# A seven-product scheme for the second weight matrix in five tiles of the last batch

## The chip, the cores and the metric

One core of a Trainium2 chip runs the kernel. The metric is the device time of one execution in microseconds (us). TensorE (PE) multiplies, VectorE (DVE) and ScalarE (ACT) work element by element and read TensorE's results in PSUM, GpSimd (POOL) works element by element in SBUF, and SyncE (SP) issues DMAs.

## What is computed

```python
X = np.fft.rfft(x, axis=1)                       # x: 8 x 3008 x 256
Yr = Xr @ w_r - Xi @ w_i + b_r                   # 256 x 256 weights
Yi = Xr @ w_i + Xi @ w_r + b_i
Y  = shrink(Yr, 0.01) + 1j * shrink(Yi, 0.01)    # soft threshold
y  = np.fft.irfft(Y, n=3008, axis=1)             # 24064 tokens of 256
h  = y @ w_in                                    # 256 x 2048
out = maximum(h, 0) ** 2 @ w_out                 # 2048 x 256
```

## The kernel before

The transform is done as matrix products in stages, each of which leaves its result in DRAM: Fwd (a folded first stage over 24 groups), Pair (second stage, mixing with the weights, threshold, and the first stage of the inverse, for two groups), and Back (the last inverse stage, for 188 tokens). Then comes the block of the two large products, in tiles of 500 or 504 tokens: six tiles for each of the eight batches, 48 in all, numbered t = 0 to 47. Batch 7, the last, has tiles 42 to 47. A tile is a raw tile (`raw[t]`, tag `yr`, one buffer) of 128 channels x 2 halves x 2h tokens (h = 250 or 252). The class Tokens prepares it on POOL: four sums and differences (tag `ms`, `sums`), and high and low halves of seven operands (`yt`, `split`; ACT writes the high half, POOL subtracts it to get the low one). Tag `ms` has one buffer, which is also that of the output tile `mo`.

Single-precision products are made of three matmuls: high by high, low by high, high by low. The product with w_in is already a seven-product scheme (Strassen's in Winograd's form): a Step (t, n), eight for each tile, computes four blocks of 128 hidden channels x h tokens from seven products of h columns. `first(n)` issues four products (12 matmuls into the banks psh0 and psh1) and four DVE instructions, `second(n)` three products (9 matmuls into psh2 and psh3) and two DVE clamps, then ACT squares the 1000 columns of `c` and copies them to the high half `g[0]`, and POOL subtracts it to get the low half `g[1]`, in two instructions of 500 columns. `out(j)` of the same step multiplies the two halves of g by w_out in the plain way: for each j six matmuls of 500 columns, accumulated over the whole tile in the two banks pso0 and pso1. After the last step ACT copies the two banks to `mo`, and two stores follow.

The order is written out by hand. Loop index m counts half steps, 16 for a tile and 96 (a slot) for a batch. Half step m = 2n issues first(n) and out(0) of step n - 2; m = 2n + 1 issues out(1) of step n - 2 and then second(n). The helper `then` keeps each engine's instructions of these calls in the order of the calls. Around them `jobs` holds the other work with due times: in the slot of batch b the pairs of batch b + 1 (twelve, 6.0 half steps apart), the first stage of batch b + 2, and, for each tile, its Back calls and its Tokens a tile ahead of use. These are placed by a planner with a cost model of its own, which fixes one order for each engine; the engines keep to that order. Loads on SP stand in a chain (`load_next`). The psf banks, two of the eight PSUM banks, serve Fwd, Pair and Back; in the last batch Back alone.

Of the kernel before, what the change touches and what calls it, by code (L numbers as in the profile page):

```python
# [38 lines left out]
}  # L39
MAIN = {  # L40
    "xt": 3, "xe": 1, "du": 1, "kv": 1, "kp": 1, "kq": 1, "ksh": 1, "ksl": 1, "kxl": 1, "kuh": 1, "kul": 1, "kb": 1, "yr": 1,
    "ms": 1, "mp": 1, "mu": 1, "mv": 1, "mc": 3, "nam": 1,
}
CONV = ("big", "small", "dw", "ds")
SIDE = ("ka", "kb", "kcm", "kxh", "kxl", "kp", "kq", "ke", "kv", "ksh", "ksl", "kuh", "kul", "ku")


# [6 lines left out]

A11, A12, A22, S1, S2, S3, S4 = range(7)
B11, B21, B22, T1, T3, T2, T4 = range(7)


@with_exitstack
def fnet_moe(ctx: ExitStack, tc, x, w_r, w_i, b2, w_in, w_out, bm, cm, dx, am2, a32, c32, d32, out):  # L60
# [19 lines left out]

    front, conv, six = ExitStack(), ExitStack(), ExitStack()
# [21 lines left out]
    def sub(eng, out, a, b):  # L105
        return eng.tensor_tensor(out=out, in0=a, in1=b, op=ALU.subtract)  # L106
# [386 lines left out]
    class Back:  # L493
# [7 lines left out]

        def load(self):
            tag = "du" if self.spans[0][0] else "mc"
            ps = slice(2 * self.q, 2 * self.q + 2)
            if self.b == 0:
                self.u = T("du", [M2, 2, D], F32, tag=tag)
                load_next(self.u, s3[0][:, ps])
                return
            self.u = T("du", [128, 3, D], F32R, tag=tag)
# [19 lines left out]
        def mm(self):  # L529
            if self.b == 0:  # L530
                return self.mm32()
            self.y = y = T("dy", [128, 2, W2], F32)
            for c in range(2):
                cs = slice(c * 128, c * 128 + 128)
                ps = bank([128, 2, 256])[:, :, :W2]
                pv = ps.rearrange("c j (p t) -> c j p t", p=2)
                mm = nc.tensor.matmul(pv[:, :, 0], self.u[:, 0, cs], dx_sb[:, 0], start=True, stop=False)  # L537

                with tc.issue_after(mm.ins):
                    nc.tensor.matmul(pv[:, :, 1], self.u[:, 1, cs], dx_sb[:, 0], start=False, stop=False)  # L540
                nc.tensor.matmul(ps[:, 0], self.u[:, 2, cs], dx_sb[:, 1], start=False, stop=True)  # L541
                self.done = copy(act, y[:, c], ps[:, 1])
                for n, (t, lo, hi, at) in enumerate(self.spans):
                    if n == c == 0 and t not in raw:
                        raw[t] = T("yr", [128, 2, 2 * HM], F32)
                    o = y[:, c, lo:hi] if n else raw[t][:, c, at:at + hi - lo]
                    self.cut = dve.tensor_add(out=o, in0=ps[:, 0, lo:hi], in1=y[:, c, lo:hi])  # L547


        def put(self):  # L550
            t, lo, hi, _ = self.spans[1]
# [62 lines left out]
                    then(dve, sub, dve, t4, y[:, 2], t2)  # L614


    acc = {}

    class Step:
        def __init__(self, t, n):  # L620
            self.t, self.n, self.h = t, n, tiles[t][2]
            self.end = t == len(tiles) - 1 and n == NF // 2 - 1

        def product(self, ps, a, b, terms=range(3)):
            yh, yl = yts[self.t]
# [35 lines left out]
        def second(self):  # L661
            h, c = self.h, self.c
            pc, pd = self.ps[2:]
            if self.end:
                return self.finish(pc, pd)
            if self.t + self.n:
                self.product(pc[:, 0], S4, B22)
                self.product(pc[:, 1], A22, T4)
                self.product(pd[:, 0], A12, B21)
            self.rectified(c[:, 1:3], pc, self.v)  # L670
            self.rectified(c[:, 0], pd[:, 0], self.p1)
            self.cut = last_of[dve]
# [8 lines left out]
            self.low = last_of[pool]  # L681

        def finish(self, pc, pd):
            h, c = self.h, self.c
# [14 lines left out]
                then(dve, sub, dve, g[1][:, j], c[:, j], g[0][:, j])  # L699

        def out(self, j):
            t, h, f = self.t, self.h, 2 * self.n + j
            if f == 0:
                acc[t] = [bank([128, 512], f"pso{d}") for d in range(2)]

            order = ((0, 0), (0, 1), (1, 0), (1, 1), (0, 2), (1, 2))
            for d, k in sorted(order, key=lambda p: p[0]) if self.end and j else order:
                w, g = ((0, 0), (1, 0), (0, 1))[k]
                then(
                    pe, pe.matmul, acc[t][d][:, :2 * h], wout[w][:, f, d * 128:(d + 1) * 128],  # L710
                    self.g[g][:, 2 * j:2 * j + 2].rearrange("p j h -> p (j h)"),
                    start=f == 0 and k == 0, stop=f == NF - 1 and k == 2,
                )
# [38 lines left out]
    def back_tasks(t, start):  # L752
        b, c0, h = tiles[t]
        new = range(-(-c0 // W2), -(-(c0 + 2 * h) // W2))
        jobs = []
        for j, q in enumerate(new):
            k, at = Back(b, q), start + 2.2 * j
            back_last[t] = k
            ahead = 1.6 if j == 0 and t > 1 and t % len(HALF) == 1 else 0.55 if j else 0.0
            jobs += [(at - ahead, k.load), (at + 1.6, (lambda k=k: behind(k.mm)) if t == 1 else k.mm)]  # L760
            if len(k.spans) > 1:
                jobs += [(start + 14.6, k.put)]
        k = Tokens(t)
# [179 lines left out]
    for m in range(2 * len(steps) + 4):  # L943
        b, r = divmod(m, slots)
        if r == 0 and b < B:
            jobs = [(t - slots, job) for t, job in jobs]
            if b + 1 < B:
                first, step, end = 1.0, 6.0, 7.1
                if b == 0:
                    first, step, end = 10.8, 5.25, 9.1  # L950
                    for q in range(EDGE, J):
                        jobs += [(0.4 + 1.2 * (q - EDGE), second[q].load)]
                        jobs += [(4.0 + 1.2 * (q - EDGE), lambda q=q: behind(second[q].run))]
                    jobs += [(0.6, lambda: part_load(parts[-2])), (2.6, lambda: part_load(parts[-1]))]
# [14 lines left out]
            steps[n - 2].out(1)  # L969
        if n < len(steps):  # L970
            (steps[n].second if k else steps[n].first)()
        if not k and 0 <= n - 2 < len(steps):
            steps[n - 2].out(0)
        if m in LATER:
            convert(LATER[m], steps[n])
        if m == max(LATER):
            conv.close()
            pools.update(dict.fromkeys(CONV), **dict.fromkeys(SIDE, memory(ctx, "side")))
        while jobs and jobs[0][0] < r + 1:
            jobs.pop(0)[1]()  # L980

# [96 lines left out]
```

## Time and profile before

| | |
|---|---|
| three runs | 2571.66 to 2572.54 us, median 2572.21 |
| profiled execution | 2572.81 us, of which the span from first to last instruction is 2571.0 |
| TensorE, DVE, ACT, POOL busy | 2562.1, 1814.9, 1394.1, 1658.6 us |
| granted TensorE clock | 1.00 of full speed |
| end of tile 41 (its output copies), 46, and of the program | 2315.1, 2529.1, 2571.0 us after the start |

A busy share over the whole run is an average over unlike stages. Matmuls overlap in TensorE, so the cost of one is read from the distance of their starts on the time line, not from its duration.

### The profile page before, as it was taken

To read this page: it belongs to the slowest core of one execution; us is meant where nothing else is said; L and a number is where in the kernel's file an instruction comes from. 1 tells how busy PE (TensorE), PEld (TensorE's weight loads), DVE (VectorE), ACT (ScalarE), POOL (GpSimd) and SP (SyncE) were. 2 spreads that over 40 slices of the span, in tenths; PEclk is the share of its full clock that TensorE was granted. 3 is DMA by queue.
4 is the path that set the end of the run, shared out by engine and by line. 5 is a ranking of instruction groups with operands and counts; after the bars stand their busy time and mean duration, and the time that the engine had idled before them with its cause. 6 is when DMAs were issued, how large, how long until landed. Compare 5 with 4: busy or idle time off the path is not lost.

```text
span 2571.0 us, 47075 instructions
## 1 busy us (share of the span) xinstructions
PE 2562.1 (100%) x17210; PEld 2359.8 (92%) x17210; DVE 1814.9 (71%) x3652; ACT 1394.1 (54%) x2128; POOL 1658.6 (65%) x1610
## 2 busy tenths in 40 slices
PE   9999999999999999999999999999999999999999
PEld 7899999999999999999999999999999999999998
DVE  7876766777767776687766877677776677765555
ACT  5655555555555555555555555555555554545443
POOL 1167666676657766677667676667767666756564
PEclk9999999999999999999999999999999999999999
DMA  9633332343323333233322333223332232211000
GB/s 313 194 94 90 115 93 83 94 121 105 93 68 106 103 106 103 62 108 101 119 88 70 103 115 114 85 61 111 104 115 76 70 92 87 67 54 53 27 24 17
DMA packets 181437, 244.66 MB, mean 95 GB/s; under 512 B 18056, under 2 KB 126592, under 8 KB 181208
## 3 DMA queue, kind: packets, MB, share of 16 engines
q1 hardware_dynamic: 167793, 216.38, 27.1%
q0 software_dynamic: 13280, 25.16, 4.0%
q8 instruction: 138, 2.26, 0.4%
q14 instruction: 91, 0.75, 0.1%
q10 hardware_dynamic: 135, 0.12, 0.0%
HBM read 144.20 MB, written 97.39 MB: 94 GB/s over the span
## 4 chain that ended last, share of the span: by engine, by line
PE 98%; DMA 1%; DVE 1%; ACT 0%; issue 0%; POOL 0%; SPq 0%; ACTq 0%; DVEq 0%
PE pso L560 41%; PE psh L560 36%; PE psf L303 7%; PE psf L282 3%; PE psf L336 2%; PE psf L244 2%; PE psf L468 1%; PE psf L541 1%; PE psf L540 1%; PE psf L537 1%; PE psf L366 1%; PE psf L518 1%; DMA x<-x_in 0%; PE psf L478 0%; PE psf L454 0%; DMA s<-xe 0%
## 5 line engine op out<-in xcount | busy, mean ns | idle before, releaser
L106 POOL TENSOR_TENSOR mg<-mc,mg 128x500 fp32r<-128x500 f32 (+1 forms) x766 | 988.4, 1311 | 551.3 <-ACT mg L102 460.1
L560 PE MATMUL pso<-mg,wout 128*128 128x500 f32 (+1 forms) x4608 | 1162.8, 391 | 0.0
L560 PE MATMUL psh<-yt,win 128*128 128x250 f32 (+1 forms) x8064 | 1067.2, 280 | 0.8 <-DVE mc L560 0.3
L560 PEld LDWEIGHTS psh<-yt,win 128*128 128x128 f32 x8064 | 1018.8, 189 | 30.6 <-DVE yt L106 0.6
L560 PEld LDWEIGHTS pso<-mg,wout 128*128 128x128 f32 x4608 | 821.9, 189 | 129.8
L560 ACT ACTIVATE mc<-mc 128x1000 f32<-128x1000 f32 (+1 forms) x384 | 400.5, 1043 | 550.3 <-DVE mc L560 549.2
L560 DVE CUSTOM_DVE_ANT_0 mc<-psh,mv 128x250 f32<-128x250 f32 (+3 forms) x769 | 418.8, 547 | 383.0 <-PE psh L560 338.6
L102 ACT CAST mg<-mc 128x1000 fp32r<-128x1000 f32 (+1 forms) x385 | 396.7, 1031 | 15.0 <-ACT mc L560 0.7
L560 DVE TENSOR_TENSOR mv<-psh,mu 128x500 f32<-128x500 f32 (+1 forms) x384 | 261.0, 680 | 43.5 <-PE psh L560 8.1
L303 PE MATMUL psf<-wx,kxh 128*128 128x256 f32 x1008 | 208.3, 281 | 0.0
L103 DVE COPY mp<-psh 128x250 f32<-128x250 f32 (+1 forms) x384 | 160.5, 418 | 52.9 <-PE psh L560 29.3
L215 POOL TENSOR_TENSOR xs<-xt 120x256 f32<-120x256 f32 x156 | 121.2, 798 | 79.3 <-DMA xt<-x_in 37.0
L560 DVE TENSOR_TENSOR mu<-psh,mp 128x250 f32<-128x250 f32 (+1 forms) x384 | 160.8, 419 | 12.1
L303 PEld LDWEIGHTS psf<-wx,kxh 128*128 128x128 f32 x1008 | 166.6, 189 | 2.7
L324 DVE TENSOR_TENSOR kv<-psf,ke 64x256 f32<-64x256 f32 x336 | 141.5, 421 | 38.9 <-PE psf L303 26.8
L560 DVE CUSTOM_DVE_ANT_0 mc<-psh,mp 128x250 f32<-128x250 f32 (+1 forms) x384 | 157.2, 409 | 6.1 <-PE psh L560 6.0
L102 ACT COPY dy<-psf 128x188 f32<-128x188 f32 (+2 forms) x229 | 70.0, 316 | 151.7 <-PE psf L541 150.9
L106 POOL TENSOR_TENSOR ksl<-kv,ksh 128x512 fp32r<-128x512 f32 x84 | 108.7, 1294 | 51.8 <-ACT ksh L102 51.6
L303 PE MATMUL psf<-wx,kxl 128*128 128x256 f32 x504 | 141.8, 281 | 0.0
L547 DVE TENSOR_TENSOR yr<-psf,dy 128x188 f32<-128x188 f32 (+2 forms) x224 | 69.0, 314 | 80.4 <-ACT dy L102 77.5
L106 POOL TENSOR_TENSOR yt<-yr,yt 128x250 fp32r<-128x250 f32 (+1 forms) x94 | 88.2, 940 | 45.7 <-ACT yt L102 45.5
L106 DVE TENSOR_TENSOR xl<-xs,xh 120x512 fp32r<-120x512 f32 x78 | 113.4, 1454 | 1.7 <-ACT xh L102 1.7
(127 smaller groups left out, 2647.7 us busy)
## 6 DMA issues: line engine op xcount, KB each, us to landing
du<-s SPq DMA_DIRECT2D x112, 256.0 KB, 2.8
ka<-s SPq DMA_DIRECT2D x96, 256.0 KB, 3.1
kcm<-cm_in POOLq DMA_DIRECT2D x84, 256.0 KB, 3.7
s<-kuh SPq DMA_DIRECT2D x84, 256.0 KB, 2.9
s<-kul SPq DMA_DIRECT2D x84, 256.0 KB, 3.5
s<-xe SPq DMA_DIRECT2D x82, 240.0 KB, 2.4
xt<-x_in SPq DMA_DIRECT2D x81, 240.0 KB, 3.2
out<-mo SPq DMA_DIRECT2D x64, 250.0 KB, 2.3
```

Of the source, the lines that this page charges most:

```text
L102: return act.copy(out=out, in_=in_)
L103: return eng.tensor_copy(out=out, in_=in_)
L106: return eng.tensor_tensor(out=out, in0=a, in1=b, op=ALU.subtract)
L215: return eng.tensor_tensor(out=out[:, :n], in0=self.xt[:, :n, 0], in1=self.xt[:, :n, 1], op=(ALU.add, ALU.subtract)[t])
L244: nc.tensor.matmul(ps[:, t], am_sb[0][:, j, t], v[:, t], start=n == 0, stop=n == 2)
L282: nc.tensor.matmul(pv[:, :, c, g, :], self.a[:, g, c * 128:(c + 1) * 128], bg, start=True, stop=True)
L303: self.last = nc.tensor.matmul(ps, l, wx[j][:, k, c, :], start=n == 0, stop=n == 5)
L324: dve.tensor_add(out=v[64 * r:64 * r + 64, g], in0=ps[gs], in1=self.e[gs, r])
L336: nc.tensor.matmul(ps[:, g], self.cm[:, g, j * 128:(j + 1) * 128], r[:, g], start=n == 0, stop=n == 2)
L366: self.mm = nc.tensor.matmul(ps[:M1, t], nam if t and i else am32[:, t], self.xt[:, 0, i], start=i == 0, stop=i == 1)
L547: self.cut = dve.tensor_add(out=o, in0=ps[:, 0, lo:hi], in1=y[:, c, lo:hi])
L560: last_of[eng] = op(*args, **kwargs)
```

## The change

For tiles 42 to 46 (`FREE`), steps 1, 3 and 5 of the eight (`SEVEN`) multiply by w_out with the seven-product scheme as well: `out_seven` issues 21 matmuls of h columns. The new operands are four sums of blocks of w_out for each of the three steps (`out_sums`, on POOL, once, in slot 6), and four sums of blocks of g for each such step (`forms`: three DVE instructions on `c` after its squaring, then high halves on ACT and low halves on POOL). Two of the seven products go straight to the pso banks and three parts into the two psf banks, which the tile keeps from step 1 on; `tile_sums` combines them on DVE after the next tile's step 0 has begun, and the final result is added to the pso banks by DVE where ACT copied them before. To have the psf banks free, all 16 Back calls of batch 7 are done in slot 6 (from half step 68.5 on), the columns of tiles 43 to 47 are stored to DRAM (`y7`), and each of these tiles is loaded again a tile ahead of its use. The pairs of batch 7 are 5.25 half steps apart instead of 6.0, and the buffers of the pair stage are given up at 68.5 for the new ones.

```diff
+ENDS = B - 1
+FREE = range(ENDS * len(HALF), B * len(HALF) - 1)
+SEVEN = (1, 3, 5)
...
     # Back.load
+            if self.b == ENDS:
+                tag = ("th", "tl")[self.q % 2]
...
     # Back.mm
-                    if n == c == 0 and t not in raw:
+                    kept = t in FREE[1:] or t > FREE[-1]
+                    if n == c == 0 and t not in raw and not kept:
                         raw[t] = T("yr", [128, 2, 2 * HM], F32)
-                    o = y[:, c, lo:hi] if n else raw[t][:, c, at:at + hi - lo]
+                    o = y[:, c, lo:hi] if n or kept else raw[t][:, c, at:at + hi - lo]
...
+            if self.b == ENDS and self.spans[-1][0] > FREE[0]:
+                lo = min(lo for t, lo, _, _ in self.spans if t > FREE[0])
+                nc.sync.dma_start(y7[:, :, W2 * self.q + lo:W2 * (self.q + 1)], y[:, :, lo:])
...
+    def out_sums(n):
...
+        pool.tensor_add(out=st[:, :512].rearrange("p (f d) -> p f d", f=2), in0=wout[0][:, 2 * n:2 * n + 2], in1=wout[1][:, 2 * n:2 * n + 2])
+        a11, a21, a12, a22 = w[:, 0, 0], w[:, 0, 1], w[:, 1, 0], w[:, 1, 1]
+        pool.tensor_add(out=s[:, 0], in0=a21, in1=a22)
+        sub(pool, s[:, 1], s[:, 0], a11)
+        sub(pool, s[:, 2], a11, a21)
+        sub(pool, s[:, 3], a12, s[:, 1])
+        halves(ws[0][:, i], ws[1][:, i], s, pool)
+
+    def tile_sums(t):
...
+        o = T("mo", [128, 4 * HM], F32, tag="ms")[:, :4 * h]
...
+        then(dve, copy, dve, s[:, 0], p16[:, 0])
+        then(dve, dve.tensor_add, out=u, in0=p16[:, 1], in1=s[:, 0])
+        then(dve, dve.tensor_add, out=s[:, 1:3], in0=p57, in1=u.unsqueeze(1).broadcast_to([128, 2, h]))
+        then(dve, dve.tensor_add, out=s[:, 3], in0=p57[:, 0], in1=s[:, 2])
...
     # Step.second
-            for j in (slice(0, 2), slice(2, 4)):
+            for j in (slice(0, 1), slice(2, 4)) if self.seven else (slice(0, 2), slice(2, 4)):
                 then(pool, sub, pool, g[1][:, j], c[:, j], g[0][:, j])
...
+        def forms(self):
...
+            then(dve, sub, dve, s[:, 0:2], c[:, 1::2], c[:, 0:2])
+            then(dve, dve.tensor_add, out=s[:, 2], in0=c[:, 0], in1=s[:, 1])
+            then(dve, sub, dve, s[:, 3], c[:, 2], s[:, 2])
+            for j in (slice(0, 2), slice(2, 4)):
+                then(act, copy, act, self.th[:, j], s[:, j])
+                then(pool, sub, pool, self.tl[:, j], s[:, j], self.th[:, j])
+
+        def out_seven(self, j):
...
+            if j == 0:
+                todo = ((p16[:, 0], plain[0], g, 0), (low[:, 0], plain[1], g, 2), (low[:, 1], sums[3], g, 3))
+            else:
+                todo = (
+                    (p57[:, 0], sums[0], tf, 0), (p57[:, 1], sums[2], tf, 1),
+                    (p16[:, 1], sums[1], tf, 2), (high[:, 0], plain[2], tf, 3),
+                )
+            for at, (ps, a, b, k) in enumerate(todo):
+                for q, (x, y) in enumerate(((0, 0), (1, 0), (0, 1))):
+                    then(
+                        pe, pe.matmul, ps, a[x], b[y][:, k],
...
     # Step.out, after the last step of a tile
-                    if d and self.end:
+                    if t in FREE:
+                        then(dve, dve.tensor_add, out=o[:, d], in0=acc[t][d][:, :2 * h], in1=o[:, d])
+                    elif d and self.end:
...
+    def raw_load(t):
+        _, c0, h = tiles[t]
+        raw[t] = T("yr", [128, 2, 2 * HM], F32)
+        load_next(raw[t][:, :, :2 * h], y7[:, :, c0:c0 + 2 * h])
+
+    def last_tasks(start, step):
+        jobs = [(start, late)]
+        for q in range(S // W2):
+            k = Back(ENDS, q)
+            jobs += [(start + 1.0 + step * max(q - 2, 0), k.load), (start + 2.6 + step * q, k.mm)]
+        return jobs + [(start + 2.0 + 5.0 * j, lambda n=n: out_sums(n)) for j, n in enumerate(SEVEN)]
...
     # the loop over half steps
+                if b + 1 == ENDS:
+                    step = 5.25
+                    jobs += last_tasks(68.5, 1.6)
                 jobs += pair_tasks(pairs[b + 1], first, step, end)
...
             (steps[n].second if k else steps[n].first)()
+            if not k and n and steps[n - 1].seven:
+                steps[n - 1].forms()
+            if not k and n % (NF // 2) == 0 and steps[n].t - 1 in FREE:
+                tile_sums(steps[n].t - 1)
```

## Rows read from the trace of the kernel before

**Rows 1.** The page, part 1: busy us, share of the span, instructions.
```profile
PE 2562.1 (100%) x17210; PEld 2359.8 (92%) x17210; DVE 1814.9 (71%) x3652; ACT 1394.1 (54%) x2128; POOL 1658.6 (65%) x1610
```

**Rows 2.** The page, part 4: the chain that ended last, by engine.
```profile
PE 98%; DMA 1%; DVE 1%; ACT 0%; issue 0%; POOL 0%; SPq 0%; ACTq 0%; DVEq 0%
```

**Rows 3.** Stretches of tiles 41, 46: busy PE, PEld, DVE, ACT, POOL; clock, DMA.
```profile
2315.10:2359.40 44.30, 44.30 (x290) 40.40 (x289) 25.85 (x58) 22.32 (x32) 29.01 (x28) 1.00 0.16 48
...
2487.80:2529.10 41.30, 41.30 (x265) 37.59 (x264) 23.51 (x48) 18.87 (x21) 24.54 (x23) 1.00 0.04 13
```

**Rows 4.** Time line, a step of tile 46: start, duration, instruction, [idle before <-releaser].
```profile
2508.44 2.60 PE L560 MATMUL psh<-yt,win 128*128 128x250 f32 x21
2509.33 0.68 DVE L560 CUSTOM_DVE_ANT_0 mc<-psh,mv 128x500 f32<-128x500 f32 x1 [1.81 <-PE psh L560]
...
2510.87 2.88 PE L560 MATMUL pso<-mg,wout 128*128 128x500 f32 x12
...
2511.41 0.68 DVE L560 TENSOR_TENSOR mv<-psh,mu 128x500 f32<-128x500 f32 x1
2511.49 1.03 ACT L102 CAST mg<-mc 128x1000 fp32r<-128x1000 f32 x1
2512.26 0.42 DVE L560 CUSTOM_DVE_ANT_0 mc<-psh,mv 128x250 f32<-128x250 f32 x1 [0.17 <-DVE mv L560]
2512.60 2.50 POOL L106 TENSOR_TENSOR mg<-mc,mg 128x500 fp32r<-128x500 f32 x2 [2.67 <-ACT mg L102]
...
2513.59 2.60 PE L560 MATMUL psh<-yt,win 128*128 128x250 f32 x21
```

**Rows 5.** Groups by line and form, POOL, 2359 to 2530 (busy us, mean ns).
```profile
L106 POOL TENSOR_TENSOR mg<-mc,mg 128x500 fp32r<-128x500 f32 x50 | 62.4, 1269 | 45.5 <-ACT mg L102 44.2 <-DVE mc L560 1.3
...
L106 POOL TENSOR_TENSOR yt<-yr,yt 128x250 fp32r<-128x250 f32 x3 | 2.2, 733 | 0.4 <-ACT yt L102 0.3
```

**Rows 6.** Groups by line and form, ACT, 2359 to 2530.
```profile
L102 ACT CAST yt<-ms 128x500 fp32r<-128x500 f32 x8 | 4.9, 612 | 4.5 <-POOL ms L106 4.5
```

**Rows 7.** Groups by line and form, DVE, whole run.
```profile
L106 DVE TENSOR_TENSOR xl<-xs,xh 120x512 fp32r<-120x512 f32 x78 | 113.4, 1454 | 1.7 <-ACT xh L102 1.7
...
L106 DVE TENSOR_TENSOR kxl<-psf,kxh 128x512 fp32r<-128x512 f32 x84 | 57.6, 685 | 35.7 <-ACT kxh L102 34.9
...
L215 DVE TENSOR_TENSOR xu<-x 120x256 f32<-120x256 f32 x6 | 2.3, 421 | 0.0
```

**Rows 8.** Time line, 446 to 449: POOL and DVE.
```profile
446.52 2.96 POOL L106 TENSOR_TENSOR mg<-mc,mg 128x504 fp32r<-128x504 f32 x2 [1.93 <-ACT mg L102]
...
447.09 1.26 DVE L106 TENSOR_TENSOR xl<-xs,xh 120x512 fp32r<-120x512 f32 x1
```

**Rows 9.** Time line, 781 to 788: POOL and DVE.
```profile
781.83 0.73 POOL L106 TENSOR_TENSOR kxl<-kp,kxh 128x256 fp32r<-128x256 f32 x1
781.84 5.31 DVE L106 TENSOR_TENSOR xl<-xs,xh 120x512 fp32r<-120x512 f32 x1
...
785.33 1.26 POOL L106 TENSOR_TENSOR yt<-ms,yt 128x504 fp32r<-128x504 f32 x1
```

**Rows 10.** Time line, 2445 to 2459: the end of tile 44.
```profile
2445.16 1.06 ACT L102 COPY mo<-pso 128x500 f32<-128x500 f32 x2 [1.18 <-PE pso L560]
...
2446.09 0.68 DVE L560 CUSTOM_DVE_ANT_0 mc<-psh,mv 128x500 f32<-128x500 f32 x1 [1.98 <-PE psh L560]
...
2448.67 1.31 POOL L106 TENSOR_TENSOR ms<-yr 128x250 f32<-128x250 f32 x2 [2.12 <-DMA out<-mo]
...
2452.39 0.63 POOL L576 TENSOR_TENSOR ms<-yr,ms 128x250 f32<-128x250 f32 x1
2452.97 1.07 POOL L106 TENSOR_TENSOR yt<-ms,yt 128x500 fp32r<-128x500 f32 x1
2454.00 0.73 POOL L106 TENSOR_TENSOR ms<-yr,ms 128x250 f32<-128x250 f32 x1
```

**Rows 11.** Groups by line, TensorE, whole run: one of three lines of Back.
```profile
L541 PE MATMUL psf<-dx_sb,du 128*128 128x188 f32 x224 | 58.5, 273 | 0.2 <-DMA du<-s 0.2
```

More of the change, by code (lines that the diff above doesn't have):

```diff
@@ L41 @@
     "xt": 3, "xe": 1, "du": 1, "kv": 1, "kp": 1, "kq": 1, "ksh": 1, "ksl": 1, "kxl": 1, "kuh": 1, "kul": 1, "kb": 1, "yr": 1,
-    "ms": 1, "mp": 1, "mu": 1, "mv": 1, "mc": 3, "nam": 1,
+    "ms": 1, "mp": 1, "mu": 1, "mv": 1, "mc": 3, "nam": 1, "wsh": 1, "wsl": 1, "tt": 1, "th": 2, "tl": 2,
 }
 CONV = ("big", "small", "dw", "ds")
+LATE = ("wsh", "wsl", "tt", "th", "tl")
 SIDE = ("ka", "kb", "kcm", "kxh", "kxl", "kp", "kq", "ke", "kv", "ksh", "ksl", "kuh", "kul", "ku")
@@ L68, in fnet_moe @@
     s3 = [dram.tile([M2 + M2 if b else M2, NP, D], F32, name=f"s3_{b}") for b in range(B)]
+    y7 = dram.tile([128, 2, S], F32, name="y7")
     am32 = const.tile([M1, 2, M1], F32, name="am32")
@@ L78, in fnet_moe @@
     dx32 = const.tile([M2, 2 * N2], F32, name="dx32")
-    front, conv, six = ExitStack(), ExitStack(), ExitStack()
+    front, conv, six, side = ExitStack(), ExitStack(), ExitStack(), ExitStack()
     def memory(stack, name, **kwargs):
@@ L508, in load @@
                 return
-            self.u = T("du", [128, 3, D], F32R, tag=tag)
+            if self.b == ENDS:
+                self.u = T("du", [128, 1024], F32R, tag=tag)[:, :3 * D].rearrange("p (k d) -> p k d", k=3)
+            else:
+                self.u = T("du", [128, 3, D], F32R, tag=tag)
             load_next(self.u[:, :2].bitcast(F32), s3[self.b][:128, ps])
@@ L614, in begin @@
                     then(dve, sub, dve, t4, y[:, 2], t2)
-    acc = {}
+    acc, part, last_sums = {}, {}, {}
+    ws = []
+    def out_sums(n):
+        if not ws:
+            ws.extend(T(name, [128, len(SEVEN), 4, 128], F32R) for name in ("wsh", "wsl"))
+        i = SEVEN.index(n)
+        st = T("st", [128, 1024], F32, tag="tt")
+        w = st[:, :512].rearrange("p (f e d) -> p f e d", f=2, e=2)
+        s = st[:, 512:].rearrange("p (j d) -> p j d", j=4)
+        pool.tensor_add(out=st[:, :512].rearrange("p (f d) -> p f d", f=2), in0=wout[0][:, 2 * n:2 * n + 2], in1=wout[1][:, 2 * n:2 * n + 2])
[6 more added lines that the diff above has]
+    def tile_sums(t):
+        h = tiles[t][2]
+        p16, p57 = part.pop(t)
+        o = T("mo", [128, 4 * HM], F32, tag="ms")[:, :4 * h]
+        s = o.rearrange("p (j h) -> p j h", j=4)
+        u = T("mu", [128, HM], F32)[:, :h]
+        then(dve, copy, dve, s[:, 0], p16[:, 0])
+        then(dve, dve.tensor_add, out=u, in0=p16[:, 1], in1=s[:, 0])
+        then(dve, dve.tensor_add, out=s[:, 1:3], in0=p57, in1=u.unsqueeze(1).broadcast_to([128, 2, h]))
+        then(dve, dve.tensor_add, out=s[:, 3], in0=p57[:, 0], in1=s[:, 2])
+        last_sums[t] = o.rearrange("p (d h) -> p d h", d=2)
     class Step:
@@ L622, in __init__ @@
             self.end = t == len(tiles) - 1 and n == NF // 2 - 1
+            self.seven = t in FREE and n in SEVEN
         def product(self, ps, a, b, terms=range(3)):
@@ L678, in second @@
             self.bent = last_of[act]
-            for j in (slice(0, 2), slice(2, 4)):
+            for j in (slice(0, 1), slice(2, 4)) if self.seven else (slice(0, 2), slice(2, 4)):
                 then(pool, sub, pool, g[1][:, j], c[:, j], g[0][:, j])
             self.low = last_of[pool]
+        def forms(self):
+            h, c = self.h, self.c
+            s, self.th, self.tl = [
+                T(f"f{name}", [128, 1024], dt, tag=name)[:, :4 * h].rearrange("p (j h) -> p j h", j=4)
+                for name, dt in (("tt", F32), ("th", F32R), ("tl", F32R))
+            ]
+            then(dve, sub, dve, s[:, 0:2], c[:, 1::2], c[:, 0:2])
[5 more added lines that the diff above has]
+        def out_seven(self, j):
+            t, h, n = self.t, self.h, self.n
+            i = SEVEN.index(n)
+            if i == j == 0:
+                part[t] = [bank([128, 512])[:, :2 * h].rearrange("p (j h) -> p j h", j=2) for _ in range(2)]
+            low, high = [a[:, :2 * h].rearrange("p (j h) -> p j h", j=2) for a in acc[t]]
+            p16, p57 = part[t]
+            f = 2 * n
+            plain = [[w[:, f + k, d * 128:(d + 1) * 128] for w in wout] for d, k in ((0, 0), (0, 1), (1, 1))]
+            sums = [[w[:, i, k] for w in ws] for k in range(4)]
+            g, tf = self.g, (self.th, self.tl)
+            if j == 0:
+                todo = ((p16[:, 0], plain[0], g, 0), (low[:, 0], plain[1], g, 2), (low[:, 1], sums[3], g, 3))
+            else:
+                todo = (
[6 more added lines that the diff above has]
+                        pe, pe.matmul, ps, a[x], b[y][:, k],
+                        start=i == q == at == 0, stop=i == len(SEVEN) - 1 and q == 2 and j == 1 and at in (1, 2),
+                    )
         def finish(self, pc, pd):
@@ L701, in out @@
         def out(self, j):
+            if self.seven:
+                return self.out_seven(j)
             t, h, f = self.t, self.h, 2 * self.n + j
@@ L715, in out @@
                 b, c0, _ = tiles[t]
-                o = T("mo", [128, 4 * HM], F32, tag="ms")[:, :4 * h].rearrange("p (d h) -> p d h", d=2)
+                if t in FREE:
+                    o = last_sums.pop(t)
+                else:
+                    o = T("mo", [128, 4 * HM], F32, tag="ms")[:, :4 * h].rearrange("p (d h) -> p d h", d=2)
                 for d in range(2):
-                    if d and self.end:
+                    if t in FREE:
+                        then(dve, dve.tensor_add, out=o[:, d], in0=acc[t][d][:, :2 * h], in1=o[:, d])
+                    elif d and self.end:
                         then(act, copy, act, o[:, d, :h], acc[t][d][:, :h])
@@ L754, in back_tasks @@
         new = range(-(-c0 // W2), -(-(c0 + 2 * h) // W2))
+        if b == ENDS:
+            new = ()
         jobs = []
@@ L762, in back_tasks @@
                 jobs += [(start + 14.6, k.put)]
+        if t > FREE[0]:
+            jobs += [(start, lambda: raw_load(t))]
         k = Tokens(t)
@@ L770, in back_tasks, with late @@
         return jobs
+    def raw_load(t):
[8 more added lines that the diff above has]
+        return jobs + [(start + 2.0 + 5.0 * j, lambda n=n: out_sums(n)) for j, n in enumerate(SEVEN)]
+    def late():
+        side.close()
+        pools.update(dict.fromkeys(LATE, memory(ctx, "late")))
     def at(items, n, *names):
@@ L977, in fnet_moe @@
             conv.close()
-            pools.update(dict.fromkeys(CONV), **dict.fromkeys(SIDE, memory(ctx, "side")))
+            pools.update(dict.fromkeys(CONV), **dict.fromkeys(SIDE, memory(side, "side")))
         while jobs and jobs[0][0] < r + 1:
```

## The prediction

> **What bounds the kernel now.** I read the page's busy times first, then its chain of waits, then the last batch tile by tile, then one step on the time line. TensorE is busy for 2562.1 of 2571.0 us, and no other engine is over 71% [rows 1]; the chain that ended last lies on TensorE for 98% [rows 2]. In the stretches of tiles 41 and 46 TensorE is busy for the whole of 44.30 and 41.30 us at a granted clock of 1.00 (its 2.4 GHz level), POOL for 29.01 and 24.54 [rows 3]. So TensorE's instruction stream sets the end, there is no stall to win back, and each new wait of TensorE counts in full. The time line of tile 46 says how late an operand may come [rows 4]. The 21 psh matmuls of 250 columns (nine of second(n), then twelve of first(n+1)) issue from 2508.44 to 2510.87, 0.1157 us each; the twelve pso matmuls of 500 columns from 2510.87 to 2513.59, 0.2267 us each. A step is 2.43 + 2.72 = 5.15 us.
>
> Measured from the end of second(n) on TensorE (2508.44 + 9 x 0.1157 = 2509.48): ACT's copy to the high half ends at 2511.49 + 1.03, 3.04 after; POOL's low halves run from 2512.60, 3.12 after, 1.25 us each; DVE has finished first(n+1) at 2512.26 + 0.42, 3.20 after [rows 4]. TensorE wants the first low half at 1.39 + 2.72 + 2.43 (first, out, then 21 psh) plus four matmuls, 7.45 after; POOL has it at 4.37. These 3.1 us are the slack of the step before the change.
>
> **What the change takes away on TensorE.** A seven-product step issues 9 + 12 = 21 matmuls of 250 columns where twelve of 500 stood: 12 x 0.2267 - 21 x 0.1157 = 0.29 us. There are 3 steps in each of 5 tiles: 15 x 0.29 = 4.4 us. The inverse stage of the last batch issues the same matmuls as before, earlier: nothing on TensorE.
>
> **What it adds, and where that lies.** In a seven-product step POOL has one low half of 250 columns (0.73, [rows 5]) in place of 500, and then two low halves of the differences, tl, of 1.25 each. These wait for ACT's high halves th (0.61, [rows 6]), and those for the three DVE instructions of forms(), which stand behind first(n+1) on DVE and can't start before 3.20. TensorE wants the first tl at 1.39 + 2.72 + 2.43 + 9 x 0.1157 + 2 x 0.1157 = 7.81, the second at 7.81 + 6 x 0.1157 = 8.51: the slack of 3.1 us is spent on a longer chain.
>
> The price that decides is that of forms(): its instructions read two operands from SBUF. Such an instruction on 512 columns takes 1454 ns on average while its twin with one operand in PSUM takes 685 ns [rows 7]. The time line shows why: at 447.09 the DVE subtraction starts under a POOL instruction that runs from 446.52; it ends 1.26 us later, 0.58 us after that POOL instruction (446.52 + 1.25 = 447.77), and POOL's pair takes 2.96 instead of the 2.50 us of an undisturbed pair [rows 4, 8]. So the DVE instruction waits for the running POOL instruction, then holds POOL up by 0.46. One on 250 columns is 685 - 421 = 0.26 us shorter [rows 7], so I take 0.20 for it. And forms() starts at 3.20, just when POOL starts its low halves at 3.12.
>
> One rule speaks against the change. The Trainium skill, "SBUF — State Buffer", section "Who interferes with whom", says that a DVE instruction with two SBUF inputs and a GpSimd instruction that reads SBUF exclude each other for a whole instruction, and that one SBUF input does not. By that rule a DVE instruction waits for at most one POOL instruction, and the sum would be the one below. The trace agrees at 447.09 but goes further at 781.84: there one subtraction took 5.31 us, and five POOL instructions ran to their end before it [rows 8, 9]; by that row a single one of the 45 forms() instructions could cost several us.
>
> *Step 5, POOL otherwise idle.* Low half 3.12 to 3.85; the first difference gets in at 3.85 and ends at 4.43; POOL's next low half 4.31 to 5.56; the second difference, which needs the first, waits to 5.56; tl one 5.76 to 7.01, in time for 7.81; the third difference waits for that, ends at 7.33; ACT to 7.94; tl two 7.94 to 9.19 where 8.51 was wanted: TensorE waits 0.68 us.
>
> *Step 1, behind the tile's end.* The final adds move from ACT (at 2445.16) to DVE: 2 x 0.68 from 2445.16 ends at 2446.52, the clamps of second() started at 2446.09 [rows 10], so they and the low halves come 0.43 later, at 3.55. On POOL the next tile's two differences ms (1.31) run ahead of them as they do now (2448.67, when the store of mo has landed, 2.4 us after its copies, [rows 10]); 0.30 later than now they end at 4.04. From there as above: low halves 4.50 and 5.43 to 6.68, tl one 6.88 to 8.13 (0.32 late), tl two to 9.38, a further 0.55 late: 0.87 us.
>
> *Step 3.* POOL still owes the next tile 0.63 + 1.07 + 0.73 and a second 1.07 = 3.5 us of sums and splits [rows 10]. Between step 2's low halves and step 3's, idle time for some 2.1 us of it is left; I take 0.68 as in step 5 and 0.2 for the overhang. If all of it goes ahead, 1.4 us more.
>
> A tile: 0.87 + 0.88 + 0.68 = 2.43 us late, less 3 x 0.29 = 0.87 won: 1.56 us slower; five tiles 7.8.
>
> **Costed at nothing, with what hides it.** tile_sums: 0.42 + 0.42 + 0.68 + 0.42 = 1.94 us on DVE (durations of the same shapes, [rows 4]) in a gap of 1.81 before the next clamp; 0.1 late, inside 3.1 us of slack; without that cover it would be 0.1 a tile. It and the adds have an operand in PSUM, so POOL isn't held. out_sums: three times about 4.6 us of POOL (two instructions of 512 columns at 1.27 and four of 128, each under the 0.63 of a 250 one, [rows 5, 10]) in tiles 40 and 41, where POOL idles 15.3 of 44.3 us [rows 3]; one instruction ahead of a low half is 1.27 late against 3.1. Without cover: 14 us. The reload of a tile is issued once the previous raw tile has been read, over 10 us ahead of its use; a store of half its size lands in 2.4 us [rows 10]. The pairs of the last batch come 5.25 half steps apart instead of 6: the same matmuls.
>
> The inverse stage goes into the last third of slot 6: three loads and a store each on SP, two copies on ACT, two to four additions on DVE, two psf banks. Raw tile 42 has one buffer, which tile 41's Tokens still read until about half step 75 of the slot, so the additions of the first Back wait there with both psf banks; queued behind them are later Backs, whose place on TensorE the planner chooses. On SP a Back load that waits for one of its four buffers, or a reload that waits for the raw tile, holds the stores of mo queued behind it, and these hold ms on POOL; the four buffers put each load three Backs ahead. The nearest row: all 224 such matmuls of the run waited 0.2 us for their data [rows 11]. Bounds 0.2 and 3 us (one POOL instruction late, 1.27, on a bank or two); I take 0 in the sum, nearest to the row, and keep 3 for the range.
>
> **The sum.** The profiled run took 2572.81 us, 1.8 over its span and 0.6 over the median of 2572.21. 2572.8 - 4.4 + 5 x 2.43 = 2580.6; I say 2580.5, 0.3% slower.
>
> **The rivals.**
> *The slack holds*: if forms() gets its three instructions in without waiting (0.68 + 0.42 + 0.42 from 3.20 ends at 4.72, tl two at 3.12 + 0.73 + 3 x 1.25 = 7.6, before 8.51), nothing is late and the time is 2572.8 - 4.4 = 2568.4. For it: 685 ns is what such an instruction takes when POOL happens to be between instructions. Against it: POOL has work back to back from 3.12 to 7.6 in every such step. It decides where a wait is under 0.3 us a step.
> *Step 1 alone is late*: if the arbitration lets DVE's second and third difference follow the first at one boundary, steps 3 and 5 are in time (0.46 + 0.20 + 0.20 added to 7.6 is 8.46), and step 1 loses about 0.9: 2572.8 - 4.4 + 5 x 0.9 = 2572.9, no change.
> *POOL's backlog*: all 3.5 us of the next tile go ahead of tl in step 3, and steps 1 and 5 as above: 1.4 - 0.2 us more a tile, 2580.6 + 6 = 2586.6; with lost arbitrations as at 781.84, 2590.
> *Faster by more than 0.2%*: that is 5.1 us, about what a measurement of this kernel can tell from no change; the matmuls give 4.4, so something else would have to end earlier, and no row shows what could.
>
> **Chances.** Forecast (2577.5 to 2585) 0.46; slack holds 0.20; step 1 alone 0.18; backlog 0.13; faster 0.03. Both middle cases lie within 0.2%: faster 0.03, same 0.38, slower 0.59. The range from 2568.4 to 2590 takes in all but the ends of the last two; the forecast's own is 2577.5 to 2585.
>
> **What would show it.** In tiles 42 to 46: twenty-one matmuls of 250 columns in place of twelve of 500 in out() of steps 1, 3 and 5; TensorE waiting for POOL's tl, 0.5 to 1 us each, some 12 us in all; forms() instructions of 0.8 to 1.8 us instead of 0.42 to 0.68; POOL low halves of about 1.7. It is wrong if the forms() instructions take their undisturbed time, if TensorE waits for something else in those tiles, or if the stretch of tiles 37 to 41 grows by more than its moved inverse stage of 13 x 6 matmuls.

## The result, and the profile after

The changed kernel takes 2586.28 us (median of four runs, 2585.36 to 2586.48); the kernel before, run beside it, 2572.38. The ratio is 1.0054 with a 95% interval of 1.0036 to 1.0071: 13.9 us slower, 5.8 us above the forecast and 1.3 us above the forecast's own range. The profiled execution took 2586.48 us with a span of 2584.7.

The page, parts 1 and 4:
```profile
PE 2567.2 (99%) x17345; PEld 2369.2 (92%) x17345; DVE 1869.0 (72%) x3727; ACT 1407.5 (54%) x2151; POOL 1706.7 (66%) x1653
...
PE 96%; DVE 2%; POOL 1%; DMA 1%; ACT 0%; issue 0%; SPq 0%; DVEq 0%; POOLq 0%; ACTq 0%
```
Against [rows 1, 2] DVE's and POOL's shares of the chain have grown from 1 and 0% to 2 and 1%, and TensorE is busy 5.1 us longer though its stream was to be 4.4 us shorter. Both have to be explained, so the next view is the last batch tile by tile: stretches from one tile's first output addition to the next, for tiles 42 to 46 (busy PE, PEld, DVE, ACT, POOL; granted clock, DMA).
```profile
2321.36:2366.34 44.98, 42.97 (x292) 39.96 (x291) 34.92 (x61) 23.39 (x28) 34.93 (x31) 0.96 0.08 24
2366.34:2409.91 43.57, 41.39 (x292) 38.39 (x291) 36.08 (x63) 22.31 (x26) 34.45 (x31) 1.00 0.08 25
2409.91:2454.19 44.28, 42.61 (x292) 39.88 (x291) 34.67 (x64) 22.20 (x26) 33.75 (x31) 0.96 0.08 25
2454.19:2498.46 44.27, 42.62 (x292) 39.89 (x291) 34.60 (x64) 22.18 (x26) 33.57 (x31) 0.96 0.08 24
2498.46:2542.77 44.31, 42.60 (x292) 39.87 (x291) 34.23 (x64) 21.39 (x24) 32.06 (x29) 0.96 0.04 13
```
Tile 46 took 41.30 us with TensorE always busy [rows 3]; now 44.31 with 1.7 us of idle. Tile 43 alone has a clock of 1.00, and a TensorE busy time that is at least 1.2 us shorter than its neighbours'. So two things are lost: idle time, and clock.

The view of waits of TensorE, 2322 to 2543 us, has one line (total, times, longest):
```profile
PE psf L574 <- POOL ftl L112: 9.1, 11, 1.6
```
Every wait is for POOL's low half of the differences (tl in the code, ftl in the trace; ftt are the three results of forms(), fth their high halves). Counted from one matmul's start to the next, less its usual 0.117, and with the 0.10 us by which the matmul after each wait is late too, the eleven waits come to 2.70, 2.97, 2.20, 2.19 and 2.24 us in tiles 42 to 46: 12.3. Step 1 has 2.32, 2.18, 2.20, 2.19 and 2.24 of it, step 3 0.39 and 0.79 in tiles 42 and 43 and nothing later, step 5 nothing. The view's 9.1 us are idle time alone; the other 3.2 us are counted as busy, since a matmul that starts late is drawn longer.

Step 1 of tile 46 on the time line (start, duration, instruction, [idle before <- releaser]):
```profile
2498.46 1.26 DVE L574 TENSOR_TENSOR mo<-pso,mo 128x500 f32<-128x500 f32 x2 [0.83 <-PE pso L574]
...
2502.06 1.31 POOL L112 TENSOR_TENSOR ms<-yr 128x250 f32<-128x250 f32 x2 [2.04 <-DMA out<-mo]
...
2503.24 0.67 DVE L112 TENSOR_TENSOR ftt<-mc 128x500 f32<-128x500 f32 x1
2503.32 2.59 POOL L112 TENSOR_TENSOR mg<-mc,mg 128x250 fp32r<-128x250 f32 x2
...
2503.95 0.83 DVE L574 TENSOR_TENSOR ftt<-mc,ftt 128x250 f32<-128x250 f32 x1
...
2504.81 1.37 DVE L112 TENSOR_TENSOR ftt<-mc,ftt 128x250 f32<-128x250 f32 x1
2505.87 0.81 POOL L590 TENSOR_TENSOR ms<-yr,ms 128x250 f32<-128x250 f32 x1
...
2506.64 1.07 POOL L112 TENSOR_TENSOR yt<-ms,yt 128x500 fp32r<-128x500 f32 x1
...
2507.67 2.46 POOL L112 TENSOR_TENSOR ftl<-ftt,fth 128x500 fp32r<-128x500 f32 x2
...
2508.96 0.38 PE L574 MATMUL psf<-ftl,wsh 128*128 128x250 f32 x1 [1.46 <-POOL ftl L112]
...
2510.18 0.38 PE L574 MATMUL psf<-ftl,wsh 128*128 128x250 f32 x1 [0.25 <-POOL ftl L112]
...
2510.75 4.15 PE L574 MATMUL psh<-yt,win 128*128 128x250 f32 x21
```
Up to POOL's low halves (mg) the order is as forecast: the additions on DVE, the two ms ahead of mg, and mg ended 6.39 us after second(n) had ended on TensorE (2498.48 + 9 x 0.1157 = 2499.52), forecast 6.68. But between mg and the first ftl stand 0.81 + 1.07 us of the next tile's sums and split; the forecast had those two behind ftl. Without them the first ftl would have been there 1.8 us earlier, and the wait that it causes is 1.62 us (2508.96 - 2507.22 - 0.12). The last line is the second loss: 21 psh matmuls reach from 2510.75 to the next out at 2514.74, 3.99 us where they took 2.43 [rows 4]. The stretches around it show why (same columns as above):
```profile
2509.00:2510.72 1.72, 1.47 (x10) 1.27 (x11) 0.41 (x1) 0.23 (x1) 1.72 (x2) 1.00 0.00 0
2510.72:2514.13 3.41, 3.41 (x18) 3.41 (x17) 1.06 (x2) 1.39 (x2) 3.41 (x4) 0.50 0.02 5
2514.13:2520.00 5.87, 5.87 (x41) 5.40 (x40) 5.35 (x10) 2.65 (x5) 3.38 (x4) 1.00 0.00 0
```
For 3.41 us the granted clock is at its 1.2 GHz level, right behind step 1's two waits (in tile 42 from the end of the second wait on). The same happens in tiles 42, 44 and 45, not in 43; each time some 1.56 us, four times 6.2. The sum by the trace: 2572.8 - 4.4 + 12.3 + 6.2 = 2586.9, where the profiled run took 2586.48. TensorE's busy time follows too: -4.4 + 6.2 + 3.2 = 5.0 us longer.

Step 5 of tile 46, where the forecast had 0.68 us of waiting and there is none:
```profile
2526.49 2.67 POOL L112 TENSOR_TENSOR mg<-mc,mg 128x250 fp32r<-128x250 f32 x2 [1.92 <-ACT mg L108]
2529.12 2.67 POOL L112 TENSOR_TENSOR ftl<-ftt,fth 128x500 fp32r<-128x500 f32 x2
...
2526.49 0.67 DVE L112 TENSOR_TENSOR ftt<-mc 128x500 f32<-128x500 f32 x1
2527.20 0.83 DVE L574 TENSOR_TENSOR ftt<-mc,ftt 128x250 f32<-128x250 f32 x1
2528.06 1.37 DVE L112 TENSOR_TENSOR ftt<-mc,ftt 128x250 f32<-128x250 f32 x1
```
DVE's first difference starts in the same instant as POOL's first low half and runs its undisturbed 0.67; POOL's is the one held up, 1.26 us where 0.73 is undisturbed. The other two differences follow at the next boundaries of POOL, one POOL instruction earlier than reckoned, so that the second ftl follows the first at once.

### The profile page after: what moved, and what is told of

Same layout as the page of the kernel before. It is cut to its first block, busy times and chain, and to the rows that moved or that the text cites. A ratio compares the mean times of both kernels' runs of the same rounds, so it can differ in the third digit from the quotient of the medians.

```text
span 2584.7 us, 47574 instructions
## 1 busy us (share of the span) xinstructions
PE 2567.2 (99%) x17345; PEld 2369.2 (92%) x17345; DVE 1869.0 (72%) x3727; ACT 1407.5 (54%) x2151; POOL 1706.7 (66%) x1653
## 4 chain that ended last, share of the span: by engine, by line
PE 96%; DVE 2%; POOL 1%; DMA 1%; ACT 0%; issue 0%; SPq 0%; DVEq 0%; POOLq 0%; ACTq 0%
PE pso L574 39%; PE psh L574 36%; PE psf L309 7%; PE psf L288 3%; PE psf L342 2%; PE psf L250 2%; PE psf L474 1%; PE psf L552 1%; PE psf L551 1%; PE psf L548 1%; PE psf L574 1%; PE psf L372 1%; POOL ftl L112 1%; PE psf L529 1%; PE psf L409 0%; PE psf L484 0%
## 5 line engine op out<-in xcount | busy, mean ns | idle before, releaser
L574 PE MATMUL pso<-mg,wout 128*128 128x500 f32 (+2 forms) x4473 | 1123.2, 390 | 0.0
L574 PEld LDWEIGHTS pso<-mg,wout 128*128 128x128 f32 x4473 | 796.5, 189 | 126.1
L332 ACT ACTIVATE kc<-kv,low 128x512 f32<-128x512 f32 x84 | 60.9, 725 | 100.4 <-DVE kv L330 100.3
```

Of the source, the lines that this page charges most:

```text
L332: act.activation(r, v, AF.Relu, bias=low)
L574: last_of[eng] = op(*args, **kwargs)
```

## The experiments

The theory after the result: nothing is lost but by TensorE waiting for ftl, because POOL comes late (its own backlog in step 1, DVE's differences between its instructions), and by what the clock does after such a wait. Rivals: the moved inverse stage costs something of its own; DVE's extra work, not POOL's order, is the cause; the clock is only a symptom that costs nothing more.

**The move alone.** The inverse stage of the last batch runs early and is kept in DRAM, and all steps use the plain scheme.
```
-            self.seven = t in FREE and n in SEVEN
+            self.seven = False
```
(with it go out_sums, tile_sums and the final additions).


> The inverse stage of the last batch is moved and kept in DRAM as in the change, the product with w_out stays plain everywhere. If the cost lies in the seven-product steps alone (POOL late with the low halves of the differences, and TensorE's clock after the long wait): 2572.4 us as before, within 1 us, and no wait of TensorE over 0.3 us in tiles 36 to 46. If the move costs too (banks held in the last third of slot 6, reloads): 1 to 3 us more than before.


Measured: 2572.26 us, ratio 1.0001 (0.9991 to 1.0010). Tile 46, same columns as in [rows 3]:
```profile
2486.98:2528.27 41.29, 41.29 (x265) 37.57 (x264) 23.51 (x48) 18.84 (x21) 24.55 (x23) 1.00 0.04 13
```
The move costs and brings nothing; all of the 13.9 us lies in the seven-product scheme, that is its steps, out_sums, tile_sums and the final additions.

**Steps 3 and 5 alone.** `SEVEN = (3, 5)`.


> Seven-product scheme in steps 3 and 5 only. If the order on POOL behind the tile's end (the next tile's sums and split ahead of the differences) is what makes step 1 late, steps 3 and 5 have small waits: 10 x 0.29 = 2.9 us won, less 0 to 0.3 us a step, so 2569.5 to 2572.5, clock at full speed throughout. If the exclusion between DVE's and POOL's instructions alone costs 0.68 us in every seven-product step, as the prediction's step 5 has it: 2572.4 - 2.9 + 10 x 0.68 = 2576.3.


Measured: 2573.01 us, 1.0005 (0.9996 to 1.0014): between the two expectations. TensorE's waits:
```profile
PE psf L574 <- POOL ftl L112: 2.4, 5, 0.5
```
Step 3 waits 0.61 to 0.67 us, and 0.10 behind it, in each tile; step 5 never does; the clock stays at 1.00. So at full clock step 3 costs about what the forecast said (0.72 to 0.77 against 0.88) and step 1 is the heavy one. The sum closes: 2572.1 less 10 x 0.29, plus 5 x 0.74, is 2572.9.

**The forms left out.** The three DVE differences are not made; th and tl come from c, so the output lacks them.
```
-            then(dve, sub, dve, s[:, 0:2], c[:, 1::2], c[:, 0:2])
-            then(dve, dve.tensor_add, out=s[:, 2], in0=c[:, 0], in1=s[:, 1])
-            then(dve, sub, dve, s[:, 3], c[:, 2], s[:, 2])
+            s = c
```


> The three DVE instructions of forms are left out: ACT and POOL split blocks of c itself instead of the four sums, so the output lacks them; the matmuls are as in the change. If DVE's waiting for POOL, and POOL's for DVE, are a main part of the lateness: waits of some 0.7 us in step 1 only (POOL still has the next tile's differences first), clock at full speed, 2572.4 - 4.4 + 3.3 = 2571.3. If POOL's own work is enough to make it late, the waits stay near 2 us a tile and the time over 2580.


Measured: 2569.82 us, 0.9990 (0.9981 to 1.0000). What is left are waits of 0.29 to 0.36 us in step 1 of each tile. POOL's low half of 250 columns, from the groups by form, and tile 46:
```profile
L112 POOL TENSOR_TENSOR mg<-mc,mg 128x250 fp32r<-128x250 f32 x9 | 6.6, 729 | 7.2 <-ACT mg L108 7.2
...
2485.23:2526.13 40.90, 40.70 (x292) 38.16 (x291) 26.44 (x54) 20.75 (x24) 30.30 (x29) 1.00 0.04 14
```
In the changed kernel the same group takes 1049 ns on average: a difference on DVE holds POOL up. TensorE's saving shows here: 40.90 - 0.46 of waits = 40.44, against 41.29 above, is 0.85 us a tile where 0.87 was reckoned. In step 1 POOL's order changed with this edit too (the split yt came behind ftl), so there it doesn't part the differences from the order. In step 3 POOL's instructions stand in the order of the changed kernel, and no wait is left; with the differences it is 0.61 to 0.67 us (steps 3 and 5 alone), so that wait is made by them.

**The next tile's sums and splits behind step 1's ftl**, by hand, with everything else as in the changed kernel.
```
...
+            jobs += [(start + 7.1 + j, lambda j=j: later(steps[8 * (t - 1) + 1].differences, lambda: k.sums(j)))]
...
```


> The next tile's sums and differences are queued on POOL behind the low halves of step 1's differences; POOL's order is otherwise the planner's (in step 3 it puts one split of 1.07 us between the two low halves). If POOL's order in step 1 decides: the wait of step 1 falls from 2.2 us to about 0.5, step 3 gets about 1 us, no single wait over 1.2 us, clock at full speed: 2572.4 - 4.4 + 5 x 1.5 = 2575.5. If the exclusion between DVE and POOL decides, step 1 keeps 1.5 us or more and the time stays over 2580.


Measured: 2578.71 us, 1.0025 (1.0016 to 1.0035): between the two expectations; 7.6 us of the 13.9 come back by the order, in part because the clock falls once only, for 6.83 us in tile 42. TensorE's waits:
```profile
PE psf L574 <- POOL ftl L112: 5.2, 11, 1.5
PE pso L574 <- POOL mg L112: 0.2, 1, 0.2
```
Step 1's wait is at most 0.21 us in four tiles of five (0.94 in tile 46), but step 3 now waits 0.85 to 2.0: what POOL still owes comes there. In tile 44's step 3 one difference lost several boundaries in a row:
```profile
2423.21 1.11 POOL L112 TENSOR_TENSOR yt<-ms,yt 128x500 fp32r<-128x500 f32 x1
...
2423.73 3.71 DVE L112 TENSOR_TENSOR ftt<-mc 128x500 f32<-128x500 f32 x1
2424.24 0.76 POOL L112 TENSOR_TENSOR ms<-yr,ms 128x250 f32<-128x250 f32 x1
2424.92 1.98 POOL L112 TENSOR_TENSOR mg<-mc,mg 128x250 fp32r<-128x250 f32 x2
...
2429.52 0.38 PE L574 MATMUL psf<-ftl,wsh 128*128 128x250 f32 x1 [0.88 <-POOL ftl L112]
```
It started under yt and ended only after four POOL instructions, 3.71 us, as the 5.31 us of [rows 9] did.

**The second half of a seven-product step half a step later**, so that ftl has more time (and tile_sums half a step later with it).
```
-            steps[n - 2].out(1)
+            if not steps[n - 2].seven:
+                steps[n - 2].out(1)
...
+            if n > 2 and steps[n - 3].seven:
+                steps[n - 3].out(1)
...
```


> The second half of a seven-product step (the four products that read th and tl) is issued one half step later, behind the first half of the next step's plain product, and the sums of a tile accordingly half a step later: 3.8 us more time for tl. If the lateness of tl is the whole loss (with the clock after it), no wait is left and 2572.4 - 4.4 = 2568.0 us. If something else in the scheme costs (DVE's load, POOL's total), it stays above 2572.


Measured: 2579.41 us, 1.0028 (1.0017 to 1.0039), not the 2568.0 that was expected if ftl's lateness were the whole loss. No wait for ftl is left, but two others are:
```profile
PE pso L574 <- POOL mg L112: 3.8, 5, 1.0
PE psh L574 <- DVE mc L574: 2.3, 5, 0.5
```
POOL's backlog isn't gone by being waited for later: the plain low half of step 2 is now what is late, and DVE's clamps, which stand behind the differences, are late for the transforms that follow.

**Both of these edits.**


> Both edits together: the next tile's sums and differences behind tl of step 1 on POOL, and the second half of a seven-product step half a step later. If POOL's backlog in steps 1 to 3 is the loss, and each edit alone only moved it (to step 3, or to step 2's plain low halves), both together leave waits of under 0.5 us a tile: 2572.1 - 4.4 + 2 = 2569.7 or less. If DVE, held up by POOL in forms, is late for psh as well (some 1 us a tile with the second half late alone): 2573 to 2575.


Measured: 2577.01 us, 1.0019 (1.0010 to 1.0027), above both expectations.
```profile
PE pso L574 <- POOL mg L112: 3.5, 5, 1.1
PE psh L574 <- DVE mc L574: 1.9, 4, 0.5
```
The wait for DVE's clamps stays in four tiles; the one for a plain low half has moved from step 2 to step 4. In tile 46 POOL works without a gap from 2496.32 until the low half of step 4 has come at 2515.03. Three seven-product steps in eight leave POOL no room from step 1 to step 4, whichever instruction is late.

**The matmuls that read only high halves first.** In the second half of each such step the eight matmuls with fth go ahead of the four with ftl; POOL's order is left.
```
...
+            if j:
+                terms.sort(key=lambda term: term[1] == 2)
...
```


> Within the second half of a seven-product step the eight matmuls that need only high halves go first, then the four that read tl. POOL's order is that of the change. tl comes 9.44 and 10.66 us after the end of second() in step 1 of tile 46; the wait of 1.6 and 0.4 us becomes two of about 0.95 us each, and the step ends 0.23 us earlier. If the half-speed clock follows from the one long wait, it is gone: 2586.3 - 6.2 - 1.2 = 2579. If it follows from the sum of the waits, it stays and the time is 2585.


Measured: 2581.43 us, 1.0037 (1.0022 to 1.0051), between the two expectations. Step 1 waits 0.86 to 1.11 and then 0.87 us, step 3 0.40 to 0.44 in the four tiles at full clock. The clock fell in one tile of five instead of four; TensorE's waits, and tiles 44 and 46:
```profile
PE psf L574 <- POOL ftl L112: 8.5, 14, 0.9
...
2407.70:2451.70 44.00, 42.54 (x292) 39.82 (x291) 34.52 (x64) 22.18 (x26) 33.79 (x31) 0.96 0.08 25
2494.68:2537.70 43.02, 41.26 (x292) 38.33 (x291) 35.62 (x63) 21.38 (x24) 32.68 (x29) 1.00 0.04 13
```
Counted from start to start as above, its waits come to 12.2 us, as in the changed kernel (12.3). Three slow stretches fewer should then save 3 x 1.56 = 4.7 us; the time is 4.9 us less. So the clock has a price of its own, beside that of the waits.

**The wait filled with work.** To part the clock from the wait, matmuls that add zero to a bank stand ahead of the first ftl matmul of step 1, thirteen of them, then six in a second kernel.
```
+                    if i == 0 and j and at == 0 and q == 2:
+                        for _ in range(13):
+                            then(pe, pe.matmul, ps[:, :128], zero, zero, start=False, stop=False)
```


> In step 1, ahead of the first matmul that reads tl, TensorE issues 13 matmuls of 128 zero columns into the same sum (1.46 us, adding zero): the wait is filled with work, the operands come as late as in the change. If the stretches at half clock (3.41 us each in four tiles, 21 psh matmuls in 3.99 instead of 2.43 us) are a cost of TensorE's pause, they go: 2586.3 - 4 x 1.56 = 2580.1. If the waits alone account for the loss and the clock does not matter, 2586 or more.

> As the filled wait before, with 6 zero matmuls in place of 13: each runs as two passes of 0.11 us, so 13 filled 2.82 us where 1.6 were open and gave the clock's gain back; 6 fill 1.3 us. If the half-speed stretches cost 4 x 1.56 us and need TensorE's pause: full speed throughout and 2586.3 - 6.2 = 2580.1. If the clock costs nothing of its own: 2586.


Measured: 2586.00 us (1.0054) with thirteen, 2583.99 us (1.0046, 1.0030 to 1.0061) with six. In both the clock stays at 1.00 in all tiles. The thirteen took longer than the wait they fill (each runs as two, 26 recorded in a tile, some 2.8 us), so that kernel tells nothing on the price. With six, tile 46 and its step 3 (POOL's low halves, then the matmul that waits):
```profile
2496.60:2540.11 43.51, 42.62 (x304) 39.70 (x303) 35.62 (x63) 21.39 (x24) 32.62 (x29) 1.00 0.04 13
...
2515.39 1.44 POOL L112 TENSOR_TENSOR ftl<-ftt,fth 128x500 fp32r<-128x500 f32 x1
...
2517.82 1.26 POOL L112 TENSOR_TENSOR ftl<-ftt,fth 128x500 fp32r<-128x500 f32 x1 [1.00 <-ACT fth L108]
...
2519.14 0.39 PE L574 MATMUL psf<-ftl,wsh 128*128 128x250 f32 x1 [0.49 <-POOL ftl L112]
```
Step 3 waits 0.61 to 0.67 us in every tile again, as it does with steps 3 and 5 alone and, with 0.69, in tile 43 of the changed kernel. So the slow stretch costs 1.56 us of TensorE, but lets POOL catch up and saves some 0.7 us of step 3; only 2.3 us of the whole come back without it. Of the 6.2 us some 2.6 go to step 3's waits, and 1.2 to an extra wait in step 1 of tile 44, where POOL began the next tile's sums 1.6 us later than in the changed kernel, counted from the output additions. The rival that the clock costs nothing falls; the 6.2 us are its gross price.

**Steps 1 and 5 alone**, with the next tile's sums behind step 1's ftl.
```
-SEVEN = (1, 3, 5)
+SEVEN = (1, 5)
```


> Seven-product scheme in steps 1 and 5 only, the next tile's sums and differences behind tl of step 1. Step 1 keeps a wait of 0.2 to 0.3 us (0.9 in the last tile, as seen with that order), step 5 none, steps 2 to 4 have POOL for the next tile: 2572.1 - 10 x 0.29 + 5 x 0.4 = 2571.2, a little below the kernel before. If the exclusion costs 0.68 us in each such step: 2576.


Measured: 2570.80 us, 0.9994 (0.9986 to 1.0003), with waits of at most 0.21 us, in step 1 alone. What POOL owes the next tile now falls into step 3, a plain one with its 3.1 us of slack.

**Steps 1 and 5, and the high halves first as well.**


> The scheme in steps 1 and 5 alone, the next tile's sums behind step 1's low differences, and in each second half the eight matmuls that read only the high parts ahead of the four that read the low parts. The theory (TensorE waits for GpSimd's low differences, and nothing else is lost): the version with the two steps and the plain order still waits 0.14 to 0.21 us and 0.10 us in step 1 of each tile; the low part is now wanted 1.1 us later for the first difference and three matmuls later for the second, so both waits go, 5 x 0.28 = 1.4 us: about 2569.4 us, 2.8 us under the kernel before, tiles of 40.8 to 40.9 us. Rival (the second difference is then what is late, or the clock takes something): no change from 2570.8 us.


Measured: 2569.72 us, 0.9990 (0.9981 to 0.9999), close to the 2569.4 expected: no wait of TensorE is left. Tile 46:
```profile
2485.14:2525.94 40.80, 40.80 (x283) 38.03 (x282) 31.81 (x60) 20.25 (x22) 30.11 (x27) 1.00 0.04 14
```
40.80 against 41.29 with the move alone is 0.49 us for two steps, where the matmuls give 0.58. It is the fastest kernel here that makes the whole product, 2.5 us or 0.1% under the one before.

## Why the prediction was right and where it was wrong

**Right: what bounds it, and the sign.** TensorE's stream sets the end, POOL's low half of the differences is what it waits for, and no other wait came up in those tiles. The saving of 0.29 us a step nearly holds (0.85 for three, 0.49 for two). The move was put at 0 of up to 3 us: shown by the move alone.

**Right in total, wrong in place: the waits.** Forecast 2.43 us a tile, 12.2 in all; measured 12.3, and that they agree is chance. The term of *step 1* was mis-sized: 0.87 us, measured 2.2. The prediction put the next tile's ms and yt behind tl there; POOL has 0.81 + 1.07 us of them ahead of it. The run with that order turned round shows it: step 1's wait falls to 0.2 in most tiles. *Step 3*: 0.88 us, measured 0.72 to 0.79 where the clock is full, and 0 to 0.39 behind a slow stretch. *Step 5*: 0.68 us, measured 0. The step that failed is "the first difference gets in at 3.85": DVE's first difference and POOL's low half became ready together and both started, so each later difference came one boundary of POOL earlier. The sizes behind it were right: POOL's pair took 2.67 instead of 1.95 us, 0.72 for two differences, where 0.46 + 0.20 was reckoned. The 685 ns that the prediction gives such an instruction when POOL is between two of its own is, in [rows 7], the time of the form with an operand in PSUM; the 0.67 us above shows that it holds for two SBUF operands as well.

**Missing: the clock.** The sum has no term for what TensorE does after a wait, and this, 6.2 us, is what lies between 2580.5 and the result, 5.8 us. A stream without pauses had a clock of 1.00 [rows 3]; with pauses of 1.55 to 1.81 and 0.40 to 0.42 us it went to half in four tiles of five. The Trainium skill, "TensorE: Matmul & The Clock Gate", section "HAM oscillation — how this bites in real kernels", tells of a loop whose waits, longer than these, bring the array back to half rate each time round. Four tiles of five agree with it in this, by their stretches at 0.50. Tile 43 (waits of 1.55 and 0.42, clock 1.00) against tile 45 (1.56 and 0.42, clock 0.50) shows that the length of the wait alone doesn't decide here; nor does it with the high halves first, where 1.11 and 0.87 us left the clock at 1.00 (tile 42) and 0.92 and 0.87 did not (tile 44).

**The rivals.** *The slack holds* is wrong for step 1; in step 5 nothing is late, as it said, though two of the three differences took 0.83 and 1.37 us. *Step 1 alone is late* is what tiles 44 to 46 look like, but at 2.2 + 1.56 us instead of 0.9, and step 3 is in time there only behind the slow stretch. *POOL's backlog* named 2586.6 us and came nearest in number; the backlog, though, stood in step 1 and not in step 3. Lost arbitrations as at 781.84 didn't occur in the changed kernel (its longest difference took 1.77 us); they did twice in other runs, the 3.71 us with the sums behind ftl and 1.93 us behind two POOL instructions with the second half later. That a DVE instruction waits for at most one POOL instruction, as the prediction drew it from the exclusion for a whole instruction in the Trainium skill ("SBUF — State Buffer", "Who interferes with whom"), fits all 45 differences of the changed kernel, and not those two.

**The signs.** TensorE's waits came, 12.3 us in all, but as single waits of 0.28 to 1.81 us instead of 0.5 to 1. The differences took 0.42 to 1.77 us where 0.8 to 1.8 was said, and POOL's low halves of 500 columns mostly 1.45 beside one, not 1.7.

What stays open: why the clock fell behind one pair of waits and not behind another nearly equal one; and whether three steps could be had with a smaller share of POOL's work at a tile's start, which wasn't tried.

## What to carry to other kernels

A scheme that saves the bound engine a little time pays only if the operands that it adds are ready: write the new chain out engine by engine, with what each queue holds in the real order of issue, not in the order that would suit. Where an engine of low average load (POOL at 66%) is in arrears in one stage, giving its result more time moves the wait to its next result; doing less there (two steps of three, with the other work put behind) all but removes it. And a wait of a dense TensorE isn't priced by its own length alone: add what the clock takes behind it.

## What the runs showed of the hardware that was not expected

The granted clock stood at half for 3.41 us behind two waits of some 2 us together in a stream that was otherwise dense, and once for 6.83 us (from 2342.75, in the kernel with the sums behind ftl). In it the psh matmuls of 250 columns start every 0.21 us instead of 0.116. Short matmuls that only add zero, in place of the wait, kept it at 1.00. When DVE and POOL start at once on SBUF operands, the loser can be POOL (1.26 us for a low half of 0.73). A matmul of 128 columns on plain f32 operands, without the fp32r type of the others, is recorded as two of 0.11 us each. And the slow stretch showed itself as time for the engine behind: it took 1.56 us from TensorE and gave POOL what made it in time for the next step.
